# A DiT block on one core: the second gate by multiply-accumulate passes on the vector engine, in place of column-tiled matmuls

## Chip, cores, metric

One core of one Trainium2 chip. The metric is the device time of one execution in microseconds (us). A time that is quoted for a kernel is the median of its runs; the profiled run is one of them. The time axis of a profile is a little shorter (248.3 us of span for a run of 250.4 us), so times are compared with times, and spans with spans. A run that is over 1.5% above the fastest of its kernel is called slow, and only fast runs are compared.

In the profiles PE is TensorE (matmuls), PEld its weight loads, DVE VectorE, ACT ScalarE, POOL GpSimd, and SP the engine that issues most DMAs. The chain of waits is the work that ended last, followed back step by step to what it waited for: time on it is time of the kernel. The granted clock is the share of its full clock at which TensorE was allowed to run.

## The reference, cut to what matters

```python
B, N, D = (2, 256, 1152); F = 4 * D                     # bf16 inputs

def reference(x, c, wqkv, wo, w_mod, w_fc1, w_fc2):
    mod = (_silu(c) @ w_mod).reshape(B, 6, 1, D)
    shift_a, scale_a, gate_a, shift_m, scale_m, gate_m = [mod[:, i] for i in range(6)]
    h = _layernorm(x) * (1 + scale_a) + shift_a
    ...                                                 # attention, output projection: a
    x = x + gate_a * a
    h2 = _layernorm(x) * (1 + scale_m) + shift_m
    m = _gelu(h2 @ w_fc1) @ w_fc2
    return x + gate_m * m
```

The case is about one of the six sections of `mod`: `gate_m = silu(c) @ w_mod[:, 5*D:6*D]`. It is a product of 2 rows with a matrix of 1152 x 1152, and it is needed only at the very end, where the output of the second feed-forward matmul is multiplied by it.

## The kernel before

The kernel runs one stage after the other on TensorE, and weights are loaded ahead into five buffers of 2.65 MB each (tag `wide`). The parts that matter here:

```python
wide = ctx.enter_context(tc.tile_pool(name="wide", bufs=5))       # the five weight buffers
# psum: tag "acc" has 6 buffers, tag "aux" 2

# ... (in this order on the DMA queue: the loads of 11 other weight tiles come first)
w_f1[2] = load_panels("w_f1_2", wfc1_v, 2 * D)
w_f1[3] = load_panels("w_f1_3", wfc1_v, 3 * D)
w_gate_m = load_section("w_gate_m", S_GATE_M)                     # 3 plain DMAs

def gate_natural(g, wg):
    pn = aux_tile([P, CTW], "pg")                                 # CTW = D // 4 = 288
    for k in range(KD):                                           # KD = 9
        for i in range(4):                                        # four column tiles, side by side
            nc.tensor.matmul(
                pn[32 * i:32 * i + B, :], sT[:, k, 0:B], wg[:, k, i * CTW:(i + 1) * CTW],
                start=(k == 0), stop=(k == KD - 1), tile_position=(0, 32 * i),
            )
    # ... four casts to bf16, four stores to gates_dram[g], then two loads that
    # ... broadcast each row of it over all 128 partitions
    return gate

# first feed-forward matmul with gelu (L658)
for m in range(MSPLIT, KF):                                       # 10 .. 35
    pacc = acc_tile([P, T], "pacc")
    for k in range(KD):
        f1_mm(pacc[:], m, k, 0, T)
    nc.scalar.activation(gT[:, m, :], pacc[:], ACT.Gelu_apprx_tanh)
    if m == 14:
        gate_m = gate_natural(1, w_gate_m)
    if m == MSPLIT:
        load_f2(0)                                                # tiles of w_fc2, into the same five buffers
    if m > MSPLIT and m % KD == KD - 1:
        load_f2(m // KD)

# second feed-forward matmul (L704): 13 output groups, 36 matmuls each
for gi, (n, t, c0, cw) in enumerate(groups):
    pacc = acc_tile([P, cw], "pacc")
    # ... 36 matmuls
    nc.vector.tensor_tensor(tmp[:], pacc[:], gate_m[:, b, c0:c0 + cw], op=ALU.mult)
    # ... + x1 on GpSimd, store
```

## Time and profile before

| what | value | read from |
|---|---|---|
| median time | 250.2 us | three runs |
| TensorE (PE) busy | 97% of the span | busy table |
| VectorE (DVE) busy | 26% | busy table |
| granted TensorE clock | 1.000 on average, 9 tenths or more in all 40 slices | cores, slices |
| the 36 gate matmuls on the chain | 1.21 us | chain of waits |
| VectorE idle | 111.6 to 180.5 us, but for 0.93 us | VectorE's timeline |

The busy table of the kernel before (busy us, share of the span, instructions):

```profile
PE 239.7 (97%) x1734; PEld 144.9 (58%) x1745; DVE 63.9 (26%) x172; ACT 69.1 (28%) x135; POOL 30.8 (12%) x46
```

The span in 40 equal slices, each digit the busy share in tenths; the stretch of the argument is slices 19 to 29:

```profile
DVE  2852551335535588720001000000001100000001
DMA  6999999999999999993194997490000000000000
```

VectorE and the DMA queues are both in use up to about slice 18. After it VectorE is almost idle, and the DMA queues are busy only in part (slices 21, 23, 24 and 27 are still full).

The chain of waits of the kernel before, from the start of the long feed-forward stage on (start us, duration us, what). Everything is TensorE's `pacc` work except the one piece `pg`, which is the gate:

```profile
111.84 11.13 PE pacc L658 x101
123.03 9.44 PE pacc L658 x43
132.47 1.21 PE pg L414 x36
133.68 0.32 PE pacc L658
...
174.57 70.30 PE pacc L704 x468
```

The instructions on the gate's weight tile (minimum, median and maximum in ns, first and last start):

```profile
L414 PE MATMUL pg<-w_gate_m,sT x36: 283/286/286, 132.4 to 133.4; 128*2 128x288 bf16 x36
```

Each of the 36 matmuls is recorded with 286 ns, and 36 times that would be 10.3 us. But the first starts at 132.4 us and the last at 133.4, and the chain gives the whole block 1.21 us: four column tiles run at the same time. What the block costs is read from the chain, not from the sum of durations.

VectorE's timeline in the same stretch (start us, us, engine, line, operation; in brackets the idle time before it and what ended it):

```profile
110.90 0.73 DVE L592 TENSOR_SCALAR hT<-pt,scale_m,shift_m 128x256 bf16<-128x256 bf16 x2 [2.61 <-PE pt L582]
133.70 0.93 DVE L422 CAST nat<-pg 2x288 bf16<-2x288 f32 x2 [22.08 <-PE pg L414]
```

From 111.6 us to the first output eviction at 180.5 us VectorE does nothing else. Finally the waits of the DMA queue (SP), in us: total, times, longest. One tile of the last weight matrix (`w_fc2`) waits for the gate's matmuls, because it is to take the buffer of the gate's section:

```profile
SPq L650 <- PE pg L414: 11.5, 1, 11.5
133.80 1.04 SPq L650 DMA_DIRECT2D w_f_1_1750<-in_w_fc_dram  x2
```

### The profile page before, as it was taken

To read this page: it belongs to the slowest core of one execution; us is meant where nothing else is said; L and a number is where in the kernel's file an instruction comes from. 1 tells how busy PE (TensorE), PEld (TensorE's weight loads), DVE (VectorE), ACT (ScalarE), POOL (GpSimd) and SP (SyncE) were. 2 spreads that over 40 slices of the span, in tenths; PEclk is the share of its full clock that TensorE was granted. 3 is DMA by queue.
4 is the path that set the end of the run, shared out by engine and by line. 5 is a ranking of instruction groups with operands and counts; after the bars stand their busy time and mean duration, and the time that the engine had idled before them with its cause. 6 is when DMAs were issued, how large, how long until landed. Compare 5 with 4: busy or idle time off the path is not lost.

```text
span 248.3 us, 4032 instructions
## 1 busy us (share of the span) xinstructions
PE 239.7 (97%) x1734; PEld 144.9 (58%) x1745; DVE 63.9 (26%) x172; ACT 69.1 (28%) x135; POOL 30.8 (12%) x46
## 2 busy tenths in 40 slices
PE   6799999999999999989999999999999999999994
PEld 2585444456657656878744444444565666656674
DVE  2852551335535588720001000000001100000001
ACT  7641341252424325593224222332000000000000
POOL 4000000021000255100003010000011122211111
PEclk9999999999999999999999999999999999999999
DMA  6999999999999999993194997490000000000000
GB/s 231 326 337 364 365 334 386 331 370 394 372 327 328 326 329 326 326 372 148 33 338 109 338 340 227 141 288 1 0 16 18 16 16 18 17 16 20 26 22 17
DMA packets 54285, 51.59 MB, mean 208 GB/s; under 512 B 1515, under 2 KB 47995, under 8 KB 54267
## 3 DMA queue, kind: packets, MB, share of 16 engines
q1 hardware_dynamic: 53664, 50.14, 64.0%
q0 software_dynamic: 576, 1.19, 1.4%
q8 instruction: 13, 0.21, 0.4%
q14 instruction: 5, 0.04, 0.1%
q10 hardware_dynamic: 27, 0.00, 0.0%
HBM read 50.14 MB, written 1.19 MB: 207 GB/s over the span
## 4 chain that ended last, share of the span: by engine, by line
PE 91%; DMA 3%; ACT 2%; DVE 1%; issue 1%; SPq 0%; ACTq 0%; DVEq 0%
PE pacc L704 28%; PE pacc L658 25%; PE pacc L488 7%; PE pacc L611 7%; PE pacc L436 7%; PE pk L265 5%; DMA w_scale_a<-in_w_mod_dram 3%; PE pk L298 2%; PE pa L544 2%; PE ps_s L464 2%; PE pn L381 1%; PE pg L414 1%; PE pm L233 1%; PE pt L243 1%; PE pt L582 1%
## 5 line engine op out<-in xcount | busy, mean ns | idle before, releaser
L704 PEld LDWEIGHTS <-gT 128*128 128x128 bf16 x468 | 44.4, 98 | 26.2
L710 DVE TENSOR_TENSOR tmp<-pacc,gate 128x384 f32<-128x384 f32 (+2 forms) x13 | 6.9, 527 | 103.8 <-PE pacc L704 103.8
L682 ACT ACTIVATE gT<-pacc 128x512 bf16<-128x512 f32 x26 | 15.5, 597 | 34.9 <-PE pacc L658 34.9
L712 POOL TENSOR_TENSOR o_sb<-tmp,x_1139 128x384 bf16<-128x384 f32 (+1 forms) x12 | 11.7, 972 | 88.9 <-DVE tmp L710 88.9
L488 PE MATMUL pacc<-w_v,hT 128*128 128x384 bf16 x108 | 19.2, 326 | 0.0
L704 PE MATMUL pacc<-w_f_2_1852,gT 128*128 128x384 bf16 (+2 forms) x117 | 18.9, 314 | 0.0
L658 PE MATMUL pacc<-hT,w_f_0_128 128*128 128x256 bf16 x162 | 18.8, 273 | 0.0
L704 PE MATMUL pacc<-w_f_1_1750,gT 128*128 128x384 bf16 x108 | 18.7, 326 | 0.0
L611 PE MATMUL pacc<-w_o,big_136 128*128 128x384 bf16 x108 | 18.5, 326 | 0.0
L704 PE MATMUL pacc<-w_f_3_1954,gT 128*128 128x384 bf16 (+2 forms) x135 | 18.4, 294 | 0.0
L704 PE MATMUL pacc<-w_f_0_1622,gT 128*128 128x384 bf16 x108 | 18.2, 326 | 0.0
L658 PE MATMUL pacc<-hT,w_f_1_132 128*128 128x512 bf16 (+1 forms) x88 | 17.9, 357 | 0.1
L436 PE MATMUL pacc<-hT,w_q 128*128 128x512 bf16 x79 | 17.7, 379 | 0.1
L658 PE MATMUL pacc<-hT,w_f_3_1047 128*128 128x512 bf16 x80 | 17.6, 379 | 0.1
L658 PE MATMUL pacc<-hT,w_f_2_1043 128*128 128x512 bf16 x79 | 17.5, 379 | 0.1
L658 PEld LDWEIGHTS <-w_f_0_128 128*128 128x128 bf16 x162 | 15.7, 98 | 1.8
L425 POOL DMA_DIRECT2D gates_dram<-nat x8 | 4.3, 543 | 79.6 <-DVE nat L422 79.6
L618 POOL TENSOR_TENSOR x_1139<-tmp,x_sb 128x384 f32<-128x384 f32 x11 | 10.0, 912 | 33.1 <-issue 27.0
L488 PEld LDWEIGHTS <-hT 128*128 128x128 bf16 x108 | 10.4, 98 | 6.3 <-issue 0.5
L611 PEld LDWEIGHTS <-big_136 128*128 128x128 bf16 x108 | 10.4, 98 | 6.2
L265 PE MATMUL pk<-big_136,w_k 128*128 128x256 bf16 (+2 forms) x88 | 13.3, 292 | 0.5 <-ACT big_136 L252 0.4
L658 PEld LDWEIGHTS <-w_f_1_132 128*128 128x128 bf16 x90 | 8.7, 98 | 8.5 <-issue 0.3
(119 smaller groups left out, 220.2 us busy)
## 6 DMA issues: line engine op xcount, KB each, us to landing
w_shift_a<-in_w_mod_dram SPq DMA_DIRECT2D x3, 864.0 KB, 11.1
w_q<-in_wqkv_dram SPq DMA_DIRECT2D x3, 864.0 KB, 12.3
w_gate_a<-in_w_mod_dram SPq DMA_DIRECT2D x3, 864.0 KB, 10.0
w_v<-in_wqkv_dram SPq DMA_DIRECT2D x3, 864.0 KB, 12.4
w_shift_m<-in_w_mod_dram SPq DMA_DIRECT2D x3, 864.0 KB, 10.2
w_scale_m<-in_w_mod_dram SPq DMA_DIRECT2D x3, 864.0 KB, 14.8
w_o<-in_wo_dram SPq DMA_DIRECT2D x3, 864.0 KB, 16.4
w_f_0_128<-in_w_fc_dram SPq DMA_DIRECT2D x3, 864.0 KB, 10.3
```

What stands on the lines that cost most here:

```text
L265: nc.tensor.matmul(pk[m][:, c0:c1], w_k[:, k, m * P:(m + 1) * P], hT0[:, k, c0:c1], start=(k == 0 and c0 == 0), stop=(k == KD - 1), skip_g ...
L298: nc.tensor.matmul(pk[m][:], w_k[:, k, m * P:(m + 1) * P], hT0[:, k, :], start=(k == 0), stop=(k == KD - 1),)
L436: nc.tensor.matmul(pacc[:], w_q[:, k, m * P:(m + 1) * P], hT[:, k, :], start=(k == 0), stop=(k == KD - 1),)
L464: nc.tensor.matmul(ps_s[:], qT[:, cc, q0:q0 + P], k_ap, start=(i == 0), stop=(i == len(chunks) - 1),)
L488: nc.tensor.matmul(pacc[:], hT[:, k, t * P:(t + 1) * P], w_v[:, k, pnl * PW:(pnl + 1) * PW], start=(k == 0), stop=(k == KD - 1),)
L611: nc.tensor.matmul(pacc[:], aT[:, k, t * P:(t + 1) * P], w_o[:, k, c0:c1], start=(k == 0), stop=(k == KD - 1),)
L618: (nc.gpsimd if pool_add else nc.vector).tensor_tensor(x1[:, t, c0:c1], tmp[:], x_sb[:, t, c0:c1], op=ALU.add)
L658: nc.tensor.matmul(dst, w_f1[m // KD][:, k, ml * P:(ml + 1) * P], hT[:, k, c0:c1], start=(k == 0), stop=(k == KD - 1),)
L682: nc.scalar.activation(gT[:, m, :], pacc[:], ACT.Gelu_apprx_tanh)
L704: nc.tensor.matmul(pacc[:], gT[:, kk, t * P:(t + 1) * P], w_f2[j][:, r, c0 - n * PW:c0 - n * PW + cw], start=(kk == 0), stop=(kk == KF - 1),)
L710: nc.vector.tensor_tensor(tmp[:], pacc[:], gate_m[:, b, c0:c0 + cw], op=ALU.mult)
L712: (nc.vector if last else nc.gpsimd).tensor_tensor(o_sb[:], tmp[:], x1[:, t, c0:c0 + cw], op=ALU.add)
```

## The change

The intent: VectorE has a hole where TensorE is the bottleneck, so the 36 matmuls are given to VectorE. For that the section is loaded transposed (output feature on the partitions, input feature along the row), `silu(c)` is broadcast over all partitions, and one `scalar_tensor_tensor` with an accumulator output makes 128 of the output features of one batch row: 9 x 2 = 18 passes of 1152 elements. The result stands in columns; a 32x32-block transpose, four small stores and the two broadcasting loads bring it into the form that was there before. The broadcast rows and the unread products lie in the buffer of the input `x`, which is free by then.

```diff
-    x_sb = act.tile([P, NT, D], BF16, name="x_sb")
+    x_sb = act.tile([P, NT, D], BF16, name="x_sb", tag="x_in")
 ...
+    s_rows = work.tile([P, KD, SW], BF16, name="s_rows", tag="s_rows", bufs=1)
+    nc.vector.transpose(s_rows[:].rearrange("p k c -> p (k c)"), sT[:].rearrange("p k c -> p (k c)"))
+    store_by_quadrant(s_dram[:].rearrange("b (k a r) -> a b k r", a=4, r=32), s_rows, B)
+
+    def dot_section(wT, s_all, spill, dst):
+        for j in range(KD):
+            for b in range(B):
+                nc.vector.scalar_tensor_tensor(
+                    spill, wT[:, j, :], 1.0, s_all[:, b, :], op0=ALU.mult, op1=ALU.mult,
+                    accum_out=dst[:, b * KD + j:b * KD + j + 1],
+                )
 ...
-    w_gate_m = load_section("w_gate_m", S_GATE_M)
+    w_gate_mT = wide_tile("w_gate_mT")
+    for r in range(0, KD, 3):
+        nc.sync.dma_start_transpose(
+            w_gate_mT[:, :, r * P:(r + 3) * P],
+            w_mod[r * P:(r + 3) * P, S_GATE_M * D:(S_GATE_M + 1) * D],
+        )
 ...
+    late = act.tile([P, NT, D], BF16, name="late", tag="x_in")
+    s_all = late[:, 0:B, :]
+    for b in range(B):
+        nc.gpsimd.dma_start(s_all[:, b, :], s_dram[b:b + 1, :].partition_broadcast(P))
+    gcol = small.tile([P, SW], FP32, name="gcol", tag="gcol", bufs=1)
+    ...
+    def gate_m_finish():
+        nc.vector.tensor_copy(gcol16[:], gcol[:])
+        nc.vector.transpose(grow16[:], gcol16[:])
+        store_by_quadrant(
+            gates_dram[1].rearrange("b (k a r) -> a (b k) r", a=4, r=32), grow16, B * KD
+        )
+        ...                                  # the two broadcasting loads, as before
 ...
         if m == 14:
-            gate_m = gate_natural(1, w_gate_m)
+            dot_section(w_gate_mT, s_all, late[:, B, :], gcol)
+            gate_m = gate_m_finish()
```

More of the change, by code (lines that the diff above doesn't have):

```diff
@@ L429, in gate_natural, with store_by_quadrant @@
         return gate
+    s_dram = tc.dram_tile([B, D], BF16, name="s_dram")
+    def store_by_quadrant(dst, src, rows):
+        for a in range(4):
+            nc.gpsimd.dma_start(dst[a], src[32 * a:32 * a + rows])
+    s_rows = work.tile([P, KD, SW], BF16, name="s_rows", tag="s_rows", bufs=1)
[8 more added lines that the diff above has]
+                )
     gate_a = None
@@ L676 @@
             fill.pop(0)()
+    late = act.tile([P, NT, D], BF16, name="late", tag="x_in")
[3 more added lines that the diff above has]
+    gcol = small.tile([P, SW], FP32, name="gcol", tag="gcol", bufs=1)
+    nc.gpsimd.memset(gcol[:], 0.0)
+    gcol16 = small.tile([P, SW], BF16, name="gcol16", tag="gcol16", bufs=1)
+    grow16 = small.tile([P, SW], BF16, name="grow16", tag="grow16", bufs=1)
+    def gate_m_finish():
[4 more added lines that the diff above has]
+        )
+        gate = act.tile([P, B, D], BF16, name="gate", tag="gate")
+        for b in range(B):
+            nc.gpsimd.dma_start(gate[:, b, :], gates_dram[1, b:b + 1, :].partition_broadcast(P))
+        return gate
     gate_m = None
```

## The prediction

> **What bounds the kernel.** TensorE. The busy table gives PE 239.7 of 248.3 us (97%), at full granted clock in every slice; the chain of waits is 91% PE. VectorE (26% busy) stands idle from 111.6 us to the first output eviction at 180.5 us, except for two gate casts at 133.7 us (its timeline). The DMA queues are full only up to about 116 us.
>
> **Removed.** The 36 column-tiled matmuls of the second gate. Each is recorded with 286 ns, but four run side by side: the chain holds all 36 as one piece of 1.20 us at 132.47 us, with matmuls directly before and behind. That piece is wholly on the critical path, so the gain is 1.2 us (0.5%), not 36 x 0.286 = 10.3 us. Four casts also go; they bound nothing.
>
> **Added.**
> - 18 multiply-accumulate passes of 1152 bf16 elements. None is in the trace. The 128x384 fp32 evictions take 558 ns[...]. [...] together 25 us, in VectorE's 69 us hole.
> - The section (2.65 MB) as three transposing DMAs. Plain, they landed in 9.6 us each, the last at about 116 us. [...] I take 10 to 35 us.
> - One early 32x32-block transpose, tiny stores, and two broadcasts of 288 KB (6.4 us to landing), which can start when the input tile is last read at 102.2 us.
>
> **Moved: the slack.** Passes start when the transposed section has landed (120 us, up to 145) and end 25 us later. From cast to landed gate took about 15 us before; so the gate is there at 160 to 185 us. Its first reader is at 180.5 us, and six accumulators give TensorE about 29 us more (5.85 us per output group). The tighter deadline: the second tile of the last weight matrix takes the section's buffer (its issue waited 11.5 us for the gate's matmuls, then went at 133.8 us) and is first multiplied at 178.8 us. Its first piece landed in 5.3 us. So the passes may end as late as about 173 us, and the transposing DMAs may take about 37 us, before TensorE waits.
>
> **Result.** 250.2 - 1.2 + about 0.1 for disturbance at 102 to 105 us, where VectorE and ScalarE are critical and GpSimd now issues broadcasts: **249.1 us**. Eight in ten: 248.5 to 252.0. Chances: faster by over 2% 0.01, within 2% 0.83, slower by over 2% 0.16.
>
> **What would show it.** No matmuls of the second gate in the groups; feed-forward matmuls without the 1.2 us piece; 18 passes of about 1.4 us on VectorE between 115 and 170 us; the second weight tile issued when the passes end, yet no wait of TensorE at the start of the last matmul stage; a PE busy sum near 238.5 us.
>
> **What would make it wrong.** [...] every us beyond about 37 us becomes a us of TensorE idle at the last weight matrix. Or passes far slower than 1.4 us. A saving above 2% is hardly possible: only 1.2 us of TensorE work goes.

The 25 us for the 18 passes is the author's estimate. It can be checked with the profile before: VectorE's evictions in the last stage take 292, 425 and 558 ns for 128, 256 and 384 fp32 elements in a row, 133 ns more for each 128. Carried on in a straight line to 1152 elements that is 1356 ns, and 18 such passes are 24.4 us. (This is an estimate too: another operation, another type, and without the accumulator read.) The 10 to 35 us for the transposing DMAs, and with it the landing at 120 us, up to 145, is a guess. The bound of about 37 us rests on the 25 us and on times of the profile.

## The result, and the profile after

The changed kernel takes 248.83 us (median of 4 runs, 248.68 to 249.43), the kernel before 250.26 us on the same chip. The ratio is 0.9949, with a 95% interval of 0.9935 to 0.9963. A ratio here is the mean time of one kernel's fast runs over that of the other's of the same rounds, so it is not quite the ratio of the medians. The change is faster by half a per cent, which is clear of noise and is called "the same" at a threshold of 2%.

The busy table of the changed kernel:

```profile
PE 238.4 (97%) x1709; PEld 144.1 (58%) x1709; DVE 88.3 (36%) x209; ACT 68.2 (28%) x133; POOL 34.3 (14%) x53
```

TensorE does 1.3 us less, VectorE 24.4 us more. The chain of waits from the start of the long stage on:

```profile
111.87 61.42 PE pacc L681 x334
173.29 70.30 PE pacc L748 x468
```

The piece `pg` is gone. From 111.84 us to 174.57 us the kernel before needed 62.73 us for this stage; now it is 61.42 us from 111.87 to 173.29: 1.31 us less. The last stage takes 70.30 us in both, so nothing is given back there. The start of the stage differs by 0.03 us, so the broadcasts that GpSimd issues at 102.7 us disturb nothing.

The added work, as the groups of instructions show it (busy us, mean ns, idle before and what ended it), and the instructions on the transposed section:

```profile
L445 DVE SCALAR_TENSOR_TENSOR late<-w_gate_mT,late 128x1152 bf16<-128x1152 bf16 x18 | 24.4, 1357 | 12.8 <-DMA w_gate_mT<-in_w_mod_dram 12.2
L445 DVE DVE_READ_ACCUMULATOR late<-w_gate_mT,late x18: 81/81/82, 125.2 to 149.0; 128x1 f32 x18
L534 SPq DMA_TRANSPOSE w_gate_mT<-in_w_mod_dram x3: 3792/3858/9735, 102.6 to 116.3; - x3
DMA to landing us min/median/max: 6.5/7.5/12.4
```

A pass took 1357 ns, with both inputs and the output in bf16. That agrees with the 1356 ns to which the evictions of the kernel before were carried on above; only this one size was run. With the accumulator read of 81 ns, which overlaps a little (1357 + 81 = 1438 ns), one pass started every 1.40 us. The passes ran from 123.9 us to 149.1 us, because the transposed section landed at 123.8 us.

The DMA queue's waits and the issue of the waiting weight tile:

```profile
SPq L673 <- DVE gcol L710: 25.5, 1, 25.5
149.10 5.74 SPq L673 DMA_DIRECT2D w_f<-in_w_fc_dram  x3
```

The tile that waited for the gate's matmuls now waits for the passes, and is issued at 149.1 us in place of 133.8. It is used from 177.7 us on (27 matmuls of 0.163 us after the last stage's start), so this is hidden. The gate's broadcast is issued at 157.7 us and its first reader comes at 179.2 us, so that is hidden too.

The DMA rate in two stretches, as stretches of the timeline (busy time of each engine, granted clock, DMA share, GB/s). The first line is the changed kernel while the transposing DMAs run alone, the second is the kernel before with plain loads just before its queues run dry:

```profile
114.00:120.00 6.00, 6.00 (x57) 5.37 (x55) 0.00 (x0) 1.79 (x3) 0.00 (x0) 1.00 1.02 219
```

```profile
108.00:114.00 6.00, 5.01 (x52) 4.39 (x50) 1.01 (x3) 4.46 (x9) 0.00 (x0) 1.00 0.99 366
```

The DMA engines were busy throughout in both (shares of 1.02 and 0.99). Transposing ran at 219 GB/s, plain loads at 366 GB/s.

### The profile page after: what moved, and what is told of

Same layout as the page of the kernel before. It is cut to its first block, busy times and chain, and to the rows that moved or that the text cites. A ratio compares the mean times of both kernels' runs of the same rounds, so it can differ in the third digit from the quotient of the medians.

```text
span 247.0 us, 4011 instructions
## 1 busy us (share of the span) xinstructions
PE 238.4 (97%) x1709; PEld 144.1 (58%) x1709; DVE 88.3 (36%) x209; ACT 68.2 (28%) x133; POOL 34.3 (14%) x53
## 4 chain that ended last, share of the span: by engine, by line
PE 90%; DMA 3%; DVE 2%; ACT 2%; issue 1%; SPq 0%; ACTq 0%; DVEq 0%
PE pacc L748 28%; PE pacc L681 26%; PE pacc L506 7%; PE pacc L454 7%; PE pacc L634 7%; PE pk L265 4%; DMA w_scale_a<-in_w_mod_dram 3%; PE pk L298 2%; PE pa L567 2%; PE ps_s L482 2%; PE pn L381 1%; DVE stats L175 1%; PE pt L605 1%; PE pm L233 1%; PE pt L243 1%
## 5 line engine op out<-in xcount | busy, mean ns | idle before, releaser
L681 PE MATMUL pacc<-hT,w_f 128*128 128x512 bf16 (+1 forms) x414 | 71.1, 333 | 0.0
L748 PE MATMUL pacc<-w_f,gT 128*128 128x384 bf16 (+2 forms) x468 | 70.5, 314 | 0.0
L681 PEld LDWEIGHTS <-w_f 128*128 128x128 bf16 x414 | 40.3, 98 | 29.4
L445 DVE SCALAR_TENSOR_TENSOR late<-w_gate_mT,late 128x1152 bf16<-128x1152 bf16 x18 | 24.4, 1357 | 12.8 <-DMA w_gate_mT<-in_w_mod_dram 12.2
L756 POOL TENSOR_TENSOR o_sb<-tmp,x 128x384 bf16<-128x384 f32 (+1 forms) x12 | 11.7, 972 | 72.5 <-DVE tmp L754 72.5
L634 PE MATMUL pacc<-w_o,big 128*128 128x384 bf16 x108 | 18.5, 326 | 0.0
L641 POOL TENSOR_TENSOR x<-tmp,x_sb 128x384 f32<-128x384 f32 x11 | 10.0, 912 | 33.0 <-issue 26.9
L634 PEld LDWEIGHTS <-big 128*128 128x128 bf16 x108 | 10.4, 98 | 6.2
L265 PE MATMUL pk<-big,w_k 128*128 128x256 bf16 (+2 forms) x90 | 13.4, 293 | 0.4 <-ACT big L252 0.4
L454 PEld LDWEIGHTS <-w_q 128*128 128x128 bf16 x81 | 7.8, 98 | 9.6 <-issue 0.3
## 6 DMA issues: line engine op xcount, KB each, us to landing
w_f<-in_w_fc_dram SPq DMA_DIRECT2D x14, 864.0 KB, 10.3
w_gate_a<-in_w_mod_dram SPq DMA_DIRECT2D x3, 864.0 KB, 10.3
```

The lines of the kernel that those rows point to most:

```text
L265: nc.tensor.matmul(pk[m][:, c0:c1], w_k[:, k, m * P:(m + 1) * P], hT0[:, k, c0:c1], start=(k == 0 and c0 == 0), stop=(k == KD - 1), skip_g ...
L445: nc.vector.scalar_tensor_tensor(spill, wT[:, j, :], 1.0, s_all[:, b, :], op0=ALU.mult, op1=ALU.mult, accum_out=dst[:, b * KD + j:b * KD + ...
L454: nc.tensor.matmul(pacc[:], w_q[:, k, m * P:(m + 1) * P], hT[:, k, :], start=(k == 0), stop=(k == KD - 1),)
L634: nc.tensor.matmul(pacc[:], aT[:, k, t * P:(t + 1) * P], w_o[:, k, c0:c1], start=(k == 0), stop=(k == KD - 1),)
L641: (nc.gpsimd if pool_add else nc.vector).tensor_tensor(x1[:, t, c0:c1], tmp[:], x_sb[:, t, c0:c1], op=ALU.add)
L681: nc.tensor.matmul(dst, w_f1[m // KD][:, k, ml * P:(ml + 1) * P], hT[:, k, c0:c1], start=(k == 0), stop=(k == KD - 1),)
```

## The experiments

The theory: the gain is the TensorE block itself, 1.3 us with all its effects, and everything that the change adds is hidden. It is hidden behind two deadlines, which the prediction named: the section's buffer (wanted by a tile of `w_fc2`), and the gate's arrival (six accumulators). The rivals: the gain comes from something else that was removed; the additions still cost something; one of the deadlines does not exist or is nearer than thought; the exchange is good wherever a block of matmuls stands. Twelve kernels ran. `e1` to `e4` shared runs of the kernel before with a median of 250.40 us.

### 1. Without any gate work

```diff
-            gate_m = gate_natural(1, w_gate_m)
+            gate_m = gate_m_stand_in        # the first gate's tile: a wrong result on purpose
```

> The kernel before without the 36 matmuls of the second gate, its casts, stores and broadcasts; the section is still loaded and the first gate stands in for the second (a wrong result on purpose). Theory (the gain is the 1.20 us piece of TensorE, and all that the change adds is hidden): 248.8 to 248.95 us, the same as the changed kernel within 0.2 us. Rival (the passes, transposes or broadcasts still cost something that eats part of the gain): clearly below the changed kernel, 248.4 us or less.

Measured: 249.34 us (5 runs, 249.15 to 249.95), ratio 0.9963. That is neither of the two: by the medians it is 0.5 us *slower* than the changed kernel, though it does less. (The two intervals, 0.9949 to 0.9977 here and 0.9935 to 0.9963 there, overlap, so the half microsecond is barely clear of noise.) The trace shows where the difference is not. TensorE's stages are the same:

```profile
111.84 61.42 PE pacc L659 x334
173.26 70.30 PE pacc L705 x468
```

Its last vector instruction ends at 244.28 us, the changed kernel's at 244.30. The excess lies after that, in the closing waits of the SP queue (total us, times, longest):

```profile
SPq L755 <- PEq L755: 1.2, 2, 1.0
```

```profile
SPq L798 <- PEq L798: 0.7, 2, 0.5
```

What follows: in the compute stages the changed kernel is as fast as one with no gate work at all, to 0.03 us at the start of the last stage. So its additions are fully hidden. The half microsecond lies at the very end of the program, in the one profiled execution of each; why it differs was not found.

### 2 and 3. The matmuls put back into the changed kernel

```diff
         if m == 14:
+            pd = aux_tile([P, CTW], "pd")
+            for rep in range(1):                     # e3: range(4)
+                for k in range(KD):
+                    for i in range(4):
+                        nc.tensor.matmul(
+                            pd[32 * i:32 * i + B, :], sT[:, k, 0:B], w_f1[3][:, k, i * CTW:(i + 1) * CTW],
+                            start=(k == 0), stop=(k == KD - 1), tile_position=(0, 32 * i),
+                        )
             dot_section(w_gate_mT, s_all, late[:, B, :], gcol)
```

> The changed kernel with 36 column-tiled matmuls of the same shape put back at the same place, on a resident section, their result unread. Theory: 250.1 us (248.83 + 1.2 to 1.3), all of the gain gone. Rival (the gain comes from something else that went, such as the four casts, the small stores, or the buffer's later release): stays at 248.8 us.

> As the run before it but with 144 such matmuls in one block. Theory: the cost is proportional, 0.03 us a matmul on TensorE: 248.83 + 4.8 to 4.9 = 253.7 us. If a fixed cost of switching between the two forms of matmul is part of the gain (the profile before hints at 0.1 us), then the first block costs 1.3 and each further one 1.2. Rival (matmuls are absorbed by a wait that hides them): less than 252 us.

Measured: 250.29 us with 36 matmuls (ratio 0.9995, interval 0.9981 to 1.0008), and 253.54 us with 144 (ratio 1.0121). One block takes back the whole gain. For the sizes take the run that has no such block (experiment 4, 248.92 us). The fast runs of `e2` have a median of 250.24 us, so the first block costs 1.3 us; four blocks cost 4.62 us, so each further one costs 1.1 us. The traces say the same: the long stage takes 61.42 us without a block (the changed kernel), 62.73 us with one (the kernel before), and 66.04 us with four (`e3`, from 111.50 to 177.54 us). In the trace of `e3` the four blocks are one piece:

```profile
111.50 20.63 PE pacc L681 x145
132.13 4.51 PE pd L731 x144
136.64 40.90 PE pacc L681 x189
177.54 70.30 PE pacc L756 x468
```

4.51 - 1.21 = 3.30 us for three more blocks, again 1.10 us each. So about 1.1 us is proportional, and about 0.2 us is paid once, however many blocks follow each other. Half of the 0.2 us lies inside the piece (1.21 us against 1.10 us). The other half lies beside it (1.31 us against 1.21 us), and that is the difference between the predicted 1.2 us and the measured 1.31 us. It is an inference from two sizes. What the 0.2 us pays for was not shown: going from one form of matmul to the other and back was not measured alone.

One execution of `e2`, the profiled one, took 512.96 us. Its recorded clock is 1.0, yet TensorE's pieces take about twice as long from beginning to end (the last stage 151.36 us). Its trace is not used, and its cause is open. The other four runs lie between 250.08 and 250.44 us.

### 4. Plain loads in place of the transposing ones

```diff
-        nc.sync.dma_start_transpose(w_gate_mT[:, :, ...], w_mod[...])
+        nc.sync.dma_start(w_gate_mT[:, r:r + 3, :], wmod_v[:, r:r + 3, S_GATE_M * D:(S_GATE_M + 1) * D])
```

> The changed kernel with the section loaded plainly in place of transposed (a wrong result on purpose); the passes read it just the same. Theory: the transposing DMAs are slower, but only within slack: the passes start at about 116 us in place of 123.9, and the time stays at 248.8 us. Rival (the transposing DMAs disturb other loads or engines): more than 0.4 us faster.

Measured: 248.92 us (ratio 0.9946, interval 0.9933 to 0.9959), against 0.9949 for the changed kernel. The passes started at 113.3 us (here the first pass needs only the first of the three loads) and ended at 138.5 us, 10.6 us earlier, and it brought nothing. So the transposing DMAs cost time only within slack, and they disturb nothing else that counts.

### 5 to 8. Longer passes: where does the slack end?

```diff
# e5: each pass twice; e6: three times
+            for rep in range(2):
                 dot_section(w_gate_mT, s_all, late[:, B, :], gcol)
# e8: 18 more passes that do not read the section; e7: 36 more
             dot_section(w_gate_mT, s_all, late[:, B, :], gcol)
+            for rep in range(1):
+                # 18 passes: s_all[:, 1 - b, :] times s_all[:, b, :], sums unread
```

> The changed kernel with each multiply-accumulate pass made twice (36 passes). Theory (the first deadline is the section's buffer, which the second tile of the last weight matrix takes): the passes end at 123.9 + 36 x 1.40 = 174.3 us, the weights' first piece lands 5.3 us later at 179.7, TensorE wants it at 177.7: a wait of about 2 us, 250.8 us (250 to 252). Rival A (the gate's arrival is the deadline; it has until about 208 us): 248.8 us. Rival B (VectorE is already nearly critical): 248.8 + 25 = 274 us.

> As many passes (36), but the second 18 read another tile, so that the section's buffer is free after the first 18. Theory: the weights come in time, the gate lands at about 174.3 + 15.9 = 190 us, before the accumulators run out at 208 us: 248.8 us. Rival B: 274 us. If this equals the run with 36 passes on the section, the buffer is not the deadline.

> 54 passes on the section. Theory: they end at 199.5 us, the weights land at 204.8, TensorE waits 27 us at the 28th matmul of its last stage: 276 us (273 to 279). Rival A: the gate lands at 215.4 us, TensorE waits about 7.6 us: 256 us.

> 54 passes, of which the last 36 read another tile, so that the section's buffer is free after 18. Theory: now the gate is the deadline: it lands at 199.5 + 15.9 = 215.4 us, the seventh output group wants an accumulator at 208.4 us: a wait of about 7.6 us, 256.4 us (254 to 259). If the buffer does not matter: the same as with 54 passes on the section.

| run | passes | median us | ratio |
|---|---|---|---|
| e5, all on the section | 36 | 248.79 | 0.9949 |
| e8, 18 on the section | 36 | 248.91 | 0.9947 |
| e6, all on the section | 54 | 249.15 | 0.9954 |
| e7, 18 on the section | 54 | 249.33 | 0.9979 |

Only e8 came out as expected. The other three missed, in one direction: 25 or even 50 us more of VectorE work cost nothing that the traces show. TensorE runs the last stage as one piece of 70.45 us, without a wait, in all four. (In e7 one of four runs took 250.73 us; its other three lie between 249.14 and 249.42. With all four, its interval is 0.9951 to 1.0007.) Two steps of my sums were wrong, and the traces say which.

First, the buffer. The waits of the DMA queue in e6:

```profile
SPq L673 <- PE pacc L681: 49.0, 4, 16.4
```

All four waits of the `w_fc2` tiles are for feed-forward matmuls now, none is for the passes. The program that reads the section longer was built with another assignment of buffers: the second `w_fc2` tile was issued at 138.8 us, into a buffer that the first feed-forward matmul had left. In e5 the section's buffer went to the last `w_fc2` tile, which was issued at 174.2 us and is wanted only some 50 us later. So these two runs did not test the deadline; they moved it out of the way. In e8 and e7 the second tile waited for the first 18 passes, as in the changed kernel, so these two did test the gate's arrival alone.

Second, the gate. I had the round trip from the last pass to the landed gate as about 16 us. In e6 and e7 it took 8 us (e6: passes end at 199.6 us, first reader at 207.9 us):

```profile
207.87 1.49 DVE L755 TENSOR_TENSOR tmp<-pacc,gate 128x384 f32<-128x384 f32 x3 [7.80 <-DMA gate<-gates_dram]
```

By then no weights are left to load. The four tiny stores (1.1 KB each) landed in 1.5 us (median) in e6 and in 5.9 us in the changed kernel, where the `w_fc2` tiles are in flight. So the gate arrived at 207.9 us, just before the accumulators ran out at about 208.4 us: the deadline was met by half a microsecond.

### 9. The first gate treated the same way

The first gate (`gate_a`) is made by the same kind of 36 matmuls, but in the attention stage. Here its section was loaded transposed as well, and its 18 passes were spread two per value group; the first gate's matmuls were taken out.

```diff
-    w_gate_a = load_section("w_gate_a", S_GATE_A)
+    w_gate_aT = wide_tile("w_gate_aT")               # three transposing DMAs
 ...
-        if m == 6:
-            gate_a = gate_natural(0, w_gate_a)
 ...
         v_group(pnl, t)
 ...
+        if i < KD:
+            gate_a_pass(i)                            # two passes
+        if i == KD - 1:
+            gate_a = gate_a_finish()
```

> The changed kernel with the first gate treated the same way: its section transposed on loading, its 18 passes spread two per value group over the attention stage, where VectorE is about half busy and the DMA queues are full. Theory (the change is free only because of VectorE's idle stretch and the free DMA queues): two passes add 2.8 us to each value group of 2.0 us, of which VectorE already uses about 1 us, so each group takes about 3.9 us: nine groups give about +17 us, less 1.3 us for the removed matmuls: about 264 us (256 to 275). Rival (a matmul block taken from TensorE is worth 1.3 us wherever it stands): 247.5 us, and then this version beats both.

Measured: 273.75 us (ratio 1.0935), which is correct and 25 us slower than the changed kernel. The direction was right and the size was not: I had expected 264 us, in a range up to 275. The chain of waits now runs through VectorE's passes, at a distance of 4.2 to 4.8 us:

```profile
62.56 1.29 DVE spill_a L467 x2
66.76 1.29 DVE spill_a L467 x2
70.96 1.29 DVE spill_a L467 x2
75.72 1.29 DVE spill_a L467 x2
```

and a stretch of this stage shows why (the columns are as above):

```profile
73.00:93.00 20.00, 14.96 (x148) 8.84 (x148) 16.91 (x37) 6.04 (x19) 0.00 (x0) 0.91 0.94 286
```

VectorE is busy for 16.9 of 20 us, against 9.7 us from 60 to 80 us in the kernel before. TensorE is the one that waits now: it is busy for 15.0 of 20 us, and its granted clock falls to 0.91. My estimate had 3.9 us for each value group; the mean distance was 4.5 us. Also, the transposing DMAs held the queue up: the value weights were issued from 50.1 us on, where the changed kernel did it from 35.3 us on, and TensorE waited for them. So a block of 1.3 us is not worth the same exchange everywhere. Here both VectorE and the DMA queue were short, and how much of the 25 us each of them cost was not separated.

### 10 and 11. Longer passes with the buffer held fixed

To test the first deadline, the section and the second `w_fc2` tile were put into a buffer of their own, together with the tiles that had been there before them.

```diff
-        return wide.tile([P, KD, D], BF16, name=name, tag="wide")
+        if name in ("w_q", "w_o", "w_gate_mT"):
+            return wide.tile([P, KD, D], BF16, name=name, tag="one", bufs=1)
+        return wide.tile([P, KD, D], BF16, name=name, tag="wide", bufs=4)
 ...
-        w = wide.tile([P, 27, PW], BF16, name=f"w_f2_{j}", tag="wide")
+        w = wide.tile([P, 27, PW], BF16, name=f"w_f2_{j}", tag="one" if j == 1 else "wide", bufs=1 if j == 1 else 4)
```

> The run with 36 passes on the section showed no loss, but its trace shows why: with longer passes, the pool gave the section's buffer to the last weight tile instead of the second. Here the buffer is fixed: the chain of tiles that share it is the one that the changed kernel had (the query weights, the output projection, the section, the second weight tile). Theory: the tile is issued at 174.4 us, its first piece lands 5.3 us later, TensorE wants it at 177.7: about 2 us lost, 250.9 us (250.2 to 252). Rival (this deadline does not exist at all): 248.9 us.

> 54 passes, the buffer fixed as in the run before. Theory: issued at 199.7 us, landed at 205, TensorE waits about 27 us in its last stage: 276 us (273 to 279), where 54 passes with the buffer chosen by the pool took 249.15. Rival: 249.2 us.

Measured: 250.21 us with 36 passes (ratio 1.0005) and 277.57 us with 54 (ratio 1.1104), where the same numbers of passes had cost nothing with the other assignment of buffers. TensorE's timeline of e10, then of e11 (in brackets the idle time before the group):

```profile
173.04 4.55 PE L753 MATMUL pacc<-w_f,gT 128*128 128x384 bf16 x27
179.77 66.06 PE L753 MATMUL pacc<-w_f,gT 128*128 128x384 bf16 x441 [2.18 <-DMA w_f<-in_w_fc_dram]
```

```profile
203.86 67.83 PE L753 MATMUL pacc<-w_f,gT 128*128 128x384 bf16 x441 [26.06 <-DMA w_f<-in_w_fc_dram]
```

TensorE stops after 27 matmuls of the last stage, exactly where the second weight tile begins, and waits 2.2 us and 26.1 us for it; I had said about 2 and 27. The tile was issued when the passes ended (174.5 and 198.8 us) and landed 5.3 and 5.0 us later. In e10 the runs other than the profiled one (251.01 us) took 250.1 to 250.3 us, so there the loss is nearer to 1.4 us. (No run has this assignment of buffers with 18 passes. But each trace has one wait of TensorE in the last stage, the one shown, and between e10 and e11 only the number of passes differs.) The deadline is real, but which tile stands under it is decided by the assignment of buffers.

### 12. Passes until the gate is late

```diff
             dot_section(w_gate_mT, s_all, late[:, B, :], gcol)
+            for rep in range(3):
+                # 18 passes that do not read the section, as in e7
```

> 72 passes, of which 54 read another tile (the buffer is free after 18), to find the gate's deadline. With 54, the gate landed at 207.9 us, 8 us after the passes and not 16, because the DMA queues were empty by then; the accumulators run out at 208.4. Theory: passes end at 224.7 us, the gate is there at 232.7, the seventh output group can start at 233.3 in place of 208.4: 25 us lost, 273.8 us (271 to 277). Rival (the gate's arrival binds nothing): 249.2 us.

Measured: 275.61 us (ratio 1.1011). TensorE's timeline:

```profile
172.69 35.26 PE L756 MATMUL pacc<-w_f,gT 128*128 128x384 bf16 x216
232.50 37.79 PE L756 MATMUL pacc<-w_f,gT 128*128 128x384 bf16 x252 [24.55 <-DVE tmp L762]
```

216 matmuls are six output groups of 36. TensorE fills the six accumulators, stops at 207.95 us, and waits 24.55 us for VectorE's first eviction, which waits for the gate. So the second deadline is where I had put it: about 29 us after the first eviction would be due. The changed kernel has its gate ready long before that.

Both e11 and e12 lost some 2 to 3 us more than their wait. The matmuls after the wait took longer: 67.83 us in e11, where e10 needs 66.06 us for the same 441, and 37.79 us in e12, where 70.30 - 35.26 = 35.04 us would be left for 252. The stretches of e12 show where (after the busy times of the five engines: granted clock, DMA share, GB/s):

```profile
208.00:233.00 25.00, 0.50 (x2) 0.26 (x2) 17.02 (x29) 0.00 (x0) 3.59 (x7) 0.54 0.08 24
233.00:243.00 10.00, 10.00 (x49) 5.46 (x48) 2.60 (x5) 0.00 (x0) 6.28 (x7) 0.78 0.20 63
243.00:253.00 10.00, 10.00 (x64) 6.00 (x62) 0.80 (x2) 0.00 (x0) 1.00 (x1) 1.00 0.06 20
```

While TensorE is idle its granted clock is 0.54 on average (in e11 too, from 178 to 206 us, nearly all of it idle), and the stretch from 233 to 243 us has 0.78. In e11 the weight loads show what that means once TensorE works again: from 203.86 to 207.34 us one starts every 0.32 us, then 47 of them take 7.65 us, 0.163 us each. So TensorE ran at half rate for about 3.5 us in e11 and at full rate after it. For e12 the same is worked out from the 0.78: if the clock was a half and then full, it was a half for 4.4 of these 10 us, to about 237.4 us, 4.9 us after TensorE started again; its weight loads show 15 gaps of 0.17 us, where those of e11 show 11. Half rate for so long loses about 2.5 us in e12 and 1.8 us in e11 (an estimate), close to the 2.75 and 1.77 us that the matmuls after the wait took longer. In e10 the clock is 1.00, and after its wait of 2.2 us the first 39 matmuls took 6.50 us, 0.167 us each. So the waits of 26.1 and 24.6 us cost more than their own length.

## Why the prediction was right

- **What bounds the kernel, and what the block is worth.** Right. The gain was put at the block's length on the chain and not at the sum of its durations. Predicted 1.2 us; 1.31 us in the trace and 1.43 us between the medians. Experiments 2 and 3 show that the block alone carries it, and that about 0.2 us of it is paid once, however many blocks follow each other. (The chain gives 1.21 us for this block; the 1.20 us of the prediction is the reading of the other gate's block.)
- **The passes.** Right: 1357 ns each, with about 1.4 us predicted; 25.2 us from first start to last end, with 25 us predicted.
- **The transposing DMAs.** The guess of 10 to 35 us was wide, and it held: from about 110 us to 123.8 us (the last load ahead of them was issued at 99.9 us, and such loads landed in 10.3 us). They are slower than plain loads, 219 against 366 GB/s, and experiment 4 shows that this costs nothing here.
- **Disturbance near 102 to 105 us.** I had added 0.1 us; there was none (0.03 us).
- **The slack.** The conclusion was right, two details were not. The second weight tile did take the section's buffer in the changed kernel, and its deadline is where I put it (experiments 10 and 11). But I took the assignment of buffers as fixed, and it is not: the program with longer passes got another one (experiments 5 and 6). And the round trip of the gate is not a constant 15 us: it was 8 us when no weights were in flight. The second deadline, the accumulators, is confirmed (experiment 12).
- **Faster by over 2%.** Excluded in advance, since only about 1.2 us of TensorE work goes. A kernel without any gate work is no faster (experiment 1).

What stays open: the half microsecond at the end of experiment 1's program, and the execution of 512.96 us. No version that was tried beats the changed kernel beyond the noise.

## What to carry to other kernels

The block of work that was taken from the bounding engine was worth about its length on the chain of waits (1.21 us), and not the sum of its durations: 36 matmuls of 286 ns each were worth 1.3 us. To move it for nothing, look for three things in the trace: a hole in the receiving engine that is long enough (here 25 us of work in a hole of 69), a DMA queue with room, and the deadline of everything that waits for the moved work, the reuse of its buffers included. The same exchange in a stage where VectorE and the DMA queue were already in use cost 25 us. And expect the assignment of buffers to change when the program changes: read it from the new trace before you count on a deadline.
